# A redrawn order for a fused attention and channel-mix kernel: first v early, five idle matmul pairs, relu and square in one step

## The chip, the cores and the metric

The kernel runs on one core of a Trainium2 chip. The metric is the time of one execution on the device in microseconds. A profile of one execution shows what each engine did: PE is the tensor engine (PEld its weight loads), DVE the vector engine, ACT the scalar engine, POOL the GpSimd engine and SP the sync engine, which here only issues DMAs.

## What is computed

Chunked attention feeds a channel mix. For 8 batches, 8 heads, 576 positions and head width 64, attention runs inside chunks of 64 positions:

```python
scores = scale * q_c @ k_c^T;  scores -= max;  attn = exp(scores);  attn /= sum + 1e-9
x = (attn @ v_c), heads side by side          # (8, 576, 512)
```

The channel mix then works on x, with x_prev the position before (zero at the start of a batch):

```python
xk = mu_k * x + (1.0 - mu_k) * x_prev
xr = mu_r * x + (1.0 - mu_r) * x_prev
k = np.maximum(xk @ w_k, 0.0)                 # w_k is 512 x 1024
v = k * k @ w_v                               # w_v is 1024 x 512
r = 1.0 / (1.0 + np.exp(-(xr @ w_r)))         # w_r is 512 x 512
return (r * v).astype(np.float32)
```

The weights arrive as 64-bit floats and are turned into 32-bit ones on the chip.

## The kernel before

The 4608 positions (8 times 576) are 18 groups g of 256. For each group the kernel loads q, k and v, turns q and k so that the head width lies on the partitions, computes scores and softmax, transposes the probabilities, multiplies them with v (which gives x already turned), mixes neighbouring positions, and forms the products with w_r, w_k and w_v. Large products are computed in f32 accuracy from two parts: each operand is split into a rounded high part and a low rest (`rounded` tiles), and three products of the four are added up (PASSES). For groups 0 to 3 these are plain products; groups 4 to 17 go in pairs p = 2 to 8 whose product with w_k (task M, tiles m) and with w_v (task V, tiles o) each take seven block products instead of eight, with sums and differences on DVE around them.

Nothing schedules the program: every step has a name, and a string ORDER of some two thousand words gives the order in which all of them are issued, with the engine behind a colon where there is a choice (A for ACT, D for DVE, G for POOL's queue). A second table, PLACE, gives each tile its address. Every engine works through its own steps in that order and waits by semaphores for the others. The words that the text uses:

- nk and nq load k and q of the first groups (lines 469 and 486), bq and bk those of later ones (531), v the values (501), sw the weights (581).
- T turns q and k on PE (tiles trq and trk, lines 649 and 673); their copies from PSUM run on ACT (line 415) or DVE (417).
- S is scores and softmax of the first groups (PE 724; maximum 746, exponential on ACT 762), Z the softmax of later groups (788 to 813, the last step at 813).
- P transposes the probabilities (tiles pt, line 841), copies them and multiplies with v (xps, 854).
- cw are the four steps that convert a block of weights: two on ACT (lines 585 and 589), two on DVE (592 and 598). hw splits it.
- Mk and Mr mix in groups 0 to 3 (938), R is the product with w_r (pr, 1140), K that with w_k (pk, 1094), V that with w_v (pv, 1173, and o, 1498).
- E is relu and square of k (lines 1075 to 1083); in the pairs these are blocks c11, c21, c22 and c12. F splits the result (1452).
- W.0 and W.1 clear a tile and run three matmuls of 512 columns on it at the start; W.2 to W.9 are FILL = 8 further steps of two idle matmuls each (line 440). Their results are used by nothing.

Of the kernel before, what the change touches and what calls it, by code (L numbers as in the profile page):

```python
# [12 lines left out]
ALU = mybir.AluOpType  # L13
# [10 lines left out]
mu.0:A nk0.0 P0.3:D W.0:D W.1 nq0.0 nk0.1:A nq0.1 nk1.0:A mu.1 T0.6 nq1.0:A mu.2:A T0.0 T0.8:A  # L24
T0.7:D T0.9 T0.2:A T0.1:D T0.3 T0.11:D T0.10:A S0.0 S0.1:D T0.5:A T0.4:A S0.2:D S0.3:A S1.0 T1.3
T1.4:A T1.5:A S1.1:D S1.2:D S1.3:A S0.4:D S0.5:D W.2 W.4 W.3 T1.0 P0.0 W.5 swr0.0 S1.4:D S1.5:D v0.0
swr1.0 cwr0.1:A T1.2:A cwr0.0:A P0.1:A T1.1:A cwr0.2:D W.6 P1.0 P0.2 dg.3 dg.1 dg.0 dg.2 v1.0 nk2.0
nq2.0 v2.0 P1.1:A cwr0.3:D S2.0 S3.0 P0.4:A cwr1.0:A cwr1.1:A S2.1:D S2.2:D Mk0.0 T2.3 P1.2 Mr0.0
swk0.0 v3.0 S2.3:A hwr0.0:A S3.1:D cwr1.2:D P1.3:D S3.2:D Mk0.1:A P1.4:A S3.3:A S2.4:D S2.5:D
Mk0.2:D T2.5:A P2.0 T2.4:A P2.1:A Mr0.1:A cwr1.3:D S3.4:D Mr0.2:D S3.5:D P2.3:D hwr1.0:A T2.0 P2.2  # L30
Mk1.0 cwk0.1:A P2.4:A cwk0.0:A T2.2:A Mk1.1:A hwr1.1:D hwr0.1:D cwk0.2:D cwk0.3:D P3.0 Mr1.0 P3.1:A
T2.1:A Mr1.1:A Mr1.2:D P3.3:D Mk1.2:D Mk2.0 hwk0.0:A P3.2 S4.0 S5.0 swk2.0 P3.4:A cwk2.0:A cwk2.1:A
hwk0.1:D Mr2.0 W.7 R01.0 swk1.0 Mk3.0:D S5.1:D Mk3.1:D cwk2.2:D Mk2.1:A cwk1.0:A cwk1.1:A S5.2:D
Mr3.0:D cwk1.2:D cwk1.3:D hwk1.0:D hwk1.1:D Mk2.2:D R01.1:A R00.0 swk3.0 bq3.1 swv3.0 bk3.0 bq3.3
bk3.1 swv0.0 Mr3.1:A cwk3.1:A cwk3.0:A R00.1:A Mr2.1:A K00.0 cwv3.1:A K00.1:A bq3.2 bk3.3 cwk3.2:D
# [286 lines left out]

PLAIN, ROUNDED = 16384, 40064
FIRST = 2
FILL = 8


class Steps:
# [1301 lines left out]
```

## Time and profile before

| | us |
|---|---|
| runs | 588.2, 586.47, 587.41 (median 587.41) |
| profiled execution | 584.91, of which the span is 583.1 |
| PE busy | 562.2 (96%) |
| DVE busy | 523.0 (90%) |
| ACT busy | 410.9 (70%) |
| POOL busy | 227.8 (39%) |

The profiled execution is one more run; its span leaves 1.8 us around it. Busy time of an engine counts instructions, not the issue of DMAs. Matmuls overlap in the engine's pipeline, so a busy PE is not PE at its peak. A releaser behind an idle time is the event that came last before the engine went on.

### The profile page before, as it was taken

To read this page: it belongs to the slowest core of one execution; us is meant where nothing else is said; L and a number is where in the kernel's file an instruction comes from. 1 tells how busy PE (TensorE), PEld (TensorE's weight loads), DVE (VectorE), ACT (ScalarE), POOL (GpSimd) and SP (SyncE) were. 2 spreads that over 40 slices of the span, in tenths; PEclk is the share of its full clock that TensorE was granted. 3 is DMA by queue.
4 is the path that set the end of the run, shared out by engine and by line. 5 is a ranking of instruction groups with operands and counts; after the bars stand their busy time and mean duration, and the time that the engine had idled before them with its cause. 6 is when DMAs were issued, how large, how long until landed. Compare 5 with 4: busy or idle time off the path is not lost.

```text
span 583.1 us, 16267 instructions
## 1 busy us (share of the span) xinstructions
PE 562.2 (96%) x6215; PEld 522.6 (90%) x6215; DVE 523.0 (90%) x878; ACT 410.9 (70%) x813; POOL 227.8 (39%) x410
## 2 busy tenths in 40 slices
PE   6889999999999999998999999999999999999996
PEld 4788998898888999997999899999998999999996
DVE  1899999889989999969998999989989998988784
ACT  2899877585675897867866875877768866946451
POOL 2400042111000035586446744257476456474710
PEclk9999999999999999999999999999999999999999
DMA  9797643443265667999769966899698746374721
GB/s 214 203 295 204 183 87 64 86 105 80 47 166 140 195 145 179 245 237 194 147 143 214 250 129 158 160 176 231 140 268 177 163 114 160 93 178 98 187 80 73
DMA packets 211453, 93.38 MB, mean 160 GB/s; under 512 B 162024, under 2 KB 201968, under 8 KB 211376
## 3 DMA queue, kind: packets, MB, share of 16 engines
q0 software_dynamic: 45824, 49.05, 33.9%
q1 hardware_dynamic: 160544, 41.46, 33.3%
q10 hardware_dynamic: 5008, 1.84, 1.5%
q8 instruction: 49, 0.80, 0.6%
q14 instruction: 28, 0.23, 0.1%
HBM read 76.55 MB, written 15.73 MB: 158 GB/s over the span
## 4 chain that ended last, share of the span: by engine, by line
PE 63%; DVE 13%; SPq 10%; DMA 6%; issue 4%; ACT 2%; POOL 1%; ACTq 1%; DVEq 0%; POOLq 0%
PE o L1498 23%; PE m L1408 12%; PE pr L1140 11%; SPq L531 8%; PE pk L1094 5%; PE pv L1173 4%; PE s L724 2%; DMA plain<-in_k 2%; PE xps L854 2%; PE pt L841 2%; DVE rounded L1452 2%; DVE plain L1422 1%; DVE plain L699 1%; DVE plain L1460 1%; SPq L529 1%
## 5 line engine op out<-in xcount | busy, mean ns | idle before, releaser
L1315 POOL DMA_DIRECT2D rounded<-kept x288 | 156.2, 549 | 153.9 <-PE pr L1140 88.3
L1498 PE MATMUL o<-rounded 128*128 128x256 f32 x1176 | 150.0, 285 | 2.7 <-DVE rounded L1452 2.3
L1498 PEld LDWEIGHTS o<-rounded 128*128 128x128 f32 x1176 | 144.2, 191 | 5.1 <-DVE rounded L1452 2.9
L1408 PE MATMUL m<-rounded 128*128 128x256 f32 x1176 | 147.4, 284 | 0.2 <-DVE plain L1422 0.2
L1408 PEld LDWEIGHTS m<-rounded 128*128 128x128 f32 x1176 | 143.7, 192 | 1.8 <-DVE plain L1422 0.6
L415 ACT ACTIVATE rounded<-plain 128x512 fp32r<-128x512 f32 (+1 forms) x158 | 100.6, 663 | 28.1 <-DVE plain L1034 9.1
L1140 PE MATMUL pr<-rounded 128*128 128x512 f32 x432 | 103.5, 392 | 0.4 <-ACT plain L1077 0.3
L501 POOL DMA_DIRECT2D plain<-in_v x76 | 47.8, 631 | 134.0 <-DMA plain<-in_k 55.5
L1140 PEld LDWEIGHTS pr<-rounded 128*128 128x128 f32 x432 | 79.5, 188 | 17.0 <-DVE rounded L1055 0.5
L1017 ACT ACTIVATE plain<-xps,mu 128x256 f32<-128x256 f32 x128 | 54.6, 490 | 21.8 <-PE xps L854 16.8
L1452 DVE TENSOR_TENSOR rounded<-plain,rounded 128x512 fp32r<-128x512 f32 x98 | 65.1, 681 | 2.0 <-PE o L1498 1.2
L1023 ACT ACTIVATE plain<-xps,mu 128x255 f32<-128x255 f32 (+3 forms) x176 | 62.5, 451 | 5.2 <-DMA out<-plain 4.7
L1173 PE MATMUL pv<-rounded 128*128 128x512 f32 x192 | 48.4, 398 | 0.7 <-DVE rounded L1116 0.7
L1094 PEld LDWEIGHTS pk<-rounded 128*128 128x128 f32 x384 | 47.2, 192 | 0.7
L699 DVE STREAM_TRANSPOSE plain<-plain 128x512 f32<-128x512 f32 x60 | 41.4, 699 | 7.1 <-DMA plain<-in_q 6.9
L1094 PE MATMUL pk<-rounded 128*128 128x256 f32 x384 | 47.6, 283 | 0.0
L1083 ACT ACTIVATE plain<-plain 128x512 f32<-128x512 f32 x64 | 39.5, 631 | 8.4 <-DVE plain L1075 7.8
L1034 DVE TENSOR_TENSOR plain<-plain 128x512 f32<-128x512 f32 x64 | 42.8, 678 | 0.4 <-ACT plain L1023 0.2
L1173 PEld LDWEIGHTS pv<-rounded 128*128 128x128 f32 x192 | 34.8, 188 | 8.2 <-DVE rounded L1116 1.5
L1460 DVE TENSOR_TENSOR plain<-plain 128x512 f32<-128x512 f32 x56 | 38.2, 687 | 1.5 <-ACT plain L1083 0.7
L415 ACT ACTIVATE plain<-m 128x512 f32<-128x512 f32 x42 | 24.2, 604 | 16.7 <-PE m L1408 13.6
L1422 DVE TENSOR_TENSOR plain<-m,plain 128x512 f32<-128x512 f32 x42 | 28.4, 681 | 6.4 <-PE m L1408 6.2
(103 smaller groups left out, 735.7 us busy)
## 6 DMA issues: line engine op xcount, KB each, us to landing
rounded<-kept POOLq DMA_DIRECT2D x288, 128.0 KB, 3.3
kept<-rounded SPq DMA_DIRECT2D x12, 512.0 KB, 3.6
out<-plain POOLq DMA_DIRECT2D x24, 256.0 KB, 3.2
plain<-in_q SPq DMA_DIRECT2D x160, 32.0 KB, 2.9
plain<-in_k SPq DMA_DIRECT2D x160, 32.0 KB, 2.4
plain<-in_v POOLq DMA_DIRECT2D x76, 64.0 KB, 2.7
plain<-in_v SPq DMA_DIRECT2D x68, 64.0 KB, 3.7
plain<-in_moe_w_k SPq DMA_DIRECT2D x4, 1024.0 KB, 6.4
```

What stands on the lines that cost most here:

```text
L415: nc.scalar.activation(to, x, AF.Copy)
L501: queue(on).dma_start(out=vt[j * CH : (j + 1) * CH, :, e, :], in_=v[b, j * HP : (j + 1) * HP, c * CH : (c + 1) * CH, :].rearrange("h t d - ...
L699: nc.vector.transpose(out=x, in_=x)
L1017: nc.scalar.activation(now(nm, h)[:, c], xps()[:, cb], AF.Copy, scale=mu2[:, 0, i, cb : cb + 1])
L1023: nc.scalar.activation(before(nm)[:, cb, s : s + n], xps()[:, cb, s - 1 : s - 1 + n], AF.Copy, scale=mu2[:, 1, i, cb : cb + 1],)
L1094: nc.tensor.matmul(pk[:, e, :], wk_at(f // 4)[:, a, cb, f % 4 * P : (f % 4 + 1) * P], x[:, b, cb, :], start=(n == 0), stop=(n == 3 * NB - 1),)
L1140: nc.tensor.matmul(pr, xr_at(g, a, cb)[:, tl * TT : (tl + 1) * TT], wr_of(g, cb // 2)[:, b, cb % 2, :], start=(n == 0), stop=(n == 3 * NB ...
L1173: nc.tensor.matmul(pv, kk_at(g, a, f // 2)[:, f % 2, tl * TT : (tl + 1) * TT], wv_at(f // 4)[:, :, b, f % 4, :], start=(f == 0 and n == 0) ...
L1315: nc.gpsimd.dma_start(out=to[:, c : c + 256], in_=of[:, c : c + 256])
L1408: nc.tensor.matmul(ps[w][:, e, :], left(n, a, cb, 2 * u + e), right(g, n, b, cb), start=first and i == 0, stop=i == 11, skip_group_check=True,
L1452: engine[e].tensor_tensor(form(p, n, u, 1), r(i), f32(form(p, n, u, 0)), ALU.subtract)
L1498: nc.tensor.matmul(ps[w][:, tl, :], form(p, n, u, a)[:, e, tl * TT : (tl + 1) * TT], moving(n, b, 2 * u + e), start=first and i == 0, stop ...
```

## The change

ORDER and PLACE are drawn anew throughout; of ORDER's table the diff shows the first line of either kernel. FILL goes from 8 to 5, so the steps W.7 to W.9 are gone. Relu and square of c11, c21 and c22 become one step `relu2`: on DVE one instruction that takes the maximum with 0 and multiplies with the tile itself, on ACT two activations, one behind the other. The block c12 keeps relu (out of PSUM) and square as two steps. Of the 42 such steps 32 run on ACT and 10 on DVE; before, 29 of the relus ran on ACT and 13 on DVE, and 37 of the squares on ACT and 5 on DVE. In c12, relu goes from 11 on ACT and 3 on DVE to 12 and 2, and square from 13 and 1 to 10 and 4. Elsewhere, steps with a choice change engine in both directions. All in all DVE has 880 instructions for 878, and ACT 779 activations for 791. Lines of the body are 6 lower up to relu2, 1 higher from there and 4 higher behind the pairs' relu step.

```diff
-mu.0:A nk0.0 P0.3:D W.0:D W.1 nq0.0 nk0.1:A nq0.1 nk1.0:A mu.1 T0.6 nq1.0:A mu.2:A T0.0 T0.8:A
...
+W.0:D W.1 mu.0:A nk0.0 nq0.0:A nk0.1 nq0.1:A v0.0 T0.6 mu.1 nk1.0 T0.7:D T0.8:D T0.0 P0.3:D T0.2:D
...
-FILL = 8
+FILL = 5
...
+    def relu2(e, x):
+        if e == "D":
+            nc.vector.scalar_tensor_tensor(out=x, in0=x, scalar=0.0, in1=x, op0=ALU.max, op1=ALU.mult)
+        else:
+            relu(e, x, x)
+            square(e, x)
+
...
         for i in ("c11", "c21", "c22", "c12"):
 
             def f_relu(e, i=i):
-                relu(e, r(i), ps[0] if i == "c12" else r(i))
+                relu(e, r(i), ps[0])
 
             def f_sq(e, i=i):
                 square(e, r(i))
 
             do.task = f"E{i}_{p}{u}"
-            do(f_relu, "AD")
-            do(f_sq, "AD")
+            if i == "c12":
+                do(f_relu, "AD")
+                do(f_sq, "AD")
+            else:
+                do(lambda e, i=i: relu2(e, r(i)), "AD")
 
```

The first place is the opening. SP's queue issues the loads; its first ten rows before are (in_k, in_q, in_v, in_moe_w_r are the inputs):

```order
L486 DMA plain<-in_k 64x4x128 x2
L486 DMA plain<-in_q 64x4x128 x4
L581 DMA plain<-in_moe_w_r 128x2x1024
L501 DMA plain<-in_v 64x4x64 x4
L581 DMA plain<-in_moe_w_r 128x2x1024
L501 DMA plain<-in_v 64x4x64 x4
L486 DMA plain<-in_k 16x4x256 x2
L486 DMA plain<-in_k 48x4x256 x2
L486 DMA plain<-in_q 16x4x256 x2
L486 DMA plain<-in_q 48x4x256 x2
```

and now:

```order
L480 DMA plain<-in_k 64x4x128 x4
L495 DMA plain<-in_v 64x4x64 x4
L463 DMA plain<-in_k 128x8x64 x2
L575 DMA plain<-in_moe_w_r 128x2x1024
L480 DMA plain<-in_k 16x4x256 x2
L480 DMA plain<-in_k 48x4x256 x2
L575 DMA plain<-in_moe_w_r 128x2x1024
L495 DMA plain<-in_v 64x4x64 x4
L480 DMA plain<-in_q 16x4x256 x2
L480 DMA plain<-in_q 48x4x256 x2
```

The first loads of v (line 501, now 495) stand directly behind the first of k, ahead of the first piece of w_r (581, now 575); the first loads of q went to ACT's queue, and the two pieces of w_r lie further apart.

On ACT, the stretch from the first exponentials (line 762, now 756) to the copies of the probabilities of group 0 (pt_0) reads before (trk and trq are turned k and q, 585 and 589 the conversion of w_r, now 579 and 583; the last number in a name counts buffers):

```order
L762 ACTIVATE plain_70<-plain_70 128x512
L415 ACTIVATE plain_70<-trk0_1_223 128x4x128
L415 ACTIVATE plain_70<-trk1_1_228 128x4x128
L762 ACTIVATE plain_70<-plain_70 128x512
L589 ACTIVATE plain_70<-plain_70 128x1024
L415 ACTIVATE plain_70<-trq1_1_258 128x4x128
L585 ACTIVATE plain_70<-plain_70 128x1024
L415 ACTIVATE plain_70<-pt_0_263 128x512
L415 ACTIVATE plain_70<-trq0_1_253 128x4x128
L415 ACTIVATE plain_70<-pt_0_263 128x512
```

and now:

```order
L756 ACTIVATE plain_70<-plain_70 128x512 x2
L409 ACTIVATE plain_70<-trk0_1_231 128x4x128
L409 ACTIVATE plain_70<-trk1_1_236 128x4x128
L409 ACTIVATE plain_70<-trq1_1_264 128x4x128
L409 ACTIVATE plain_70<-pt_0_274 128x512
L583 ACTIVATE plain_70<-plain_70 128x1024
L579 ACTIVATE plain_70<-plain_70 128x1024
L409 ACTIVATE plain_70<-xps_0_291 128x4x128
```

The two conversions, which stood ahead of the copy of pt_0, stand behind it, and the copy of trq0_1 is no longer among ACT's rows here.

The second place is the transposes of group 4's probabilities (pt_4, rows of line 841, now 835) on PE. Before (pk and pv are products with w_k and w_v of the group named by the first number, warm6 is an idle pair):

```order
L1094 MATMUL pk_2_3_1709<-rounded_71 128x256 x24
L440 MATMUL warm6_1734<-plain_70 128x128 x2
L1173 MATMUL pv_2_0_1737<-rounded_71 128x512 x6
L1173 MATMUL pv_2_1_1744<-rounded_71 128x512 x9
L1094 MATMUL pk_3_1_1758<-rounded_71 128x256 x24
L1173 MATMUL pv_2_0_1737<-rounded_71 128x512 x3
L841 MATMUL pt_4_1803<-ident_72,plain_70 128x128 x4
L1173 MATMUL pv_2_1_1744<-rounded_71 128x512 x3
L841 MATMUL pt_4_1803<-ident_72,plain_70 128x128 x4
```

and now (pr is the product with w_r):

```order
L1141 MATMUL pr_2_0_1614<-rounded_71 128x512 x12
L1141 MATMUL pr_2_1_1673<-rounded_71 128x512 x12
L1095 MATMUL pk_2_3_1706<-rounded_71 128x256 x24
L1174 MATMUL pv_2_0_1741<-rounded_71 128x512 x3
L1174 MATMUL pv_2_1_1745<-rounded_71 128x512 x6
L1174 MATMUL pv_2_0_1741<-rounded_71 128x512 x3
L1095 MATMUL pk_3_0_1758<-rounded_71 128x256 x24
L835 MATMUL pt_4_1791<-ident_72,plain_70 128x128 x8
```

The idle pair is gone, the products with w_r of group 2 stand nearer to the transposes, and all eight transposes come together. Ahead of the first of them PE has 1018 matmuls, where it had 1028.

On DVE, the softmax that those transposes wait for ends with the row of line 813 (now 807; zg_4 holds group 4's sums and their reciprocals). Before:

```order
L1208 TENSOR_TENSOR plain_70<-rounded_71 128x512
L1214 TENSOR_TENSOR plain_70<-plain_70 128x512
L807 TENSOR_REDUCE zg_4_1784<-plain_70 128x16
L808 TENSOR_SCALAR zg_4_1784<-zg_4_1784 128x16
L809 RECIPROCAL zg_4_1784<-zg_4_1784 128x16
L1007 TENSOR_TENSOR plain_70<-last_2_1376,mu2_78 128x4
L813 TENSOR_TENSOR plain_70<-plain_70,zg_4_1784 128x1024
```

and now:

```order
L1237 TENSOR_TENSOR rounded_71<-plain_70,rounded_71 128x512
L693 STREAM_TRANSPOSE plain_70<-plain_70 128x4x128
L801 TENSOR_REDUCE zg_4_1737<-plain_70 128x16
L802 TENSOR_SCALAR zg_4_1737<-zg_4_1737 128x16
L803 RECIPROCAL zg_4_1737<-zg_4_1737 128x16
L1117 TENSOR_TENSOR rounded_71<-plain_70,rounded_71 128x512
L411 CAST rounded_71<-plain_70 128x512
L807 TENSOR_TENSOR plain_70<-plain_70,zg_4_1737 128x1024
```

Two steps of other groups stand between the reciprocal and the last step, where there was one. Up to and with that last step DVE has 179 instructions, where it had 172.

## Rows read from the trace of the kernel before

**Rows 1.** The page, part 1: busy time, share and instructions of an engine.
```profile
PE 562.2 (96%) x6215; PEld 522.6 (90%) x6215; DVE 523.0 (90%) x878; ACT 410.9 (70%) x813; POOL 227.8 (39%) x410
```

**Rows 2.** By stretch: length, busy time (instructions) of each engine, PEclk, DMA share, GB/s.
```profile
5.87:12.40 6.53, 2.81 (x128) 2.53 (x131) 1.28 (x3) 2.64 (x6) 1.96 (x4) 0.95 1.18 281
...
30.00:44.10 14.10, 12.70 (x267) 11.83 (x268) 12.87 (x20) 14.10 (x19) 0.00 (x0) 1.00 0.96 311
44.10:100.00 55.90, 55.90 (x464) 50.42 (x463) 54.14 (x81) 47.13 (x76) 10.10 (x16) 1.00 0.57 136
100.00:133.00 33.00, 33.00 (x329) 29.76 (x328) 28.59 (x47) 21.73 (x43) 4.96 (x8) 1.00 0.43 89
133.00:275.00 142.00, 136.57 (x1492) 124.78 (x1491) 132.54 (x228) 103.49 (x219) 43.55 (x77) 1.00 0.69 163
275.00:447.00 172.00, 169.50 (x1927) 160.69 (x1925) 163.09 (x280) 126.31 (x264) 94.94 (x173) 1.00 0.88 182
447.00:578.40 131.40, 131.34 (x1278) 126.62 (x1278) 115.28 (x197) 82.51 (x170) 63.73 (x116) 1.00 0.53 128
```

**Rows 3.** What PE waits for from 44 us on: total us, times, longest.
```profile
PE o L1498 <- DVE rounded L1452: 2.3, 3, 1.9
PE xps L854 <- DMA plain<-in_v: 1.1, 1, 1.1
```

**Rows 4.** Timeline of the opening: start, duration, engine, line, operation, tiles, [idle before].
```profile
8.73 1.28 ACT L550 ACT_TABLE_LOAD   x1 [8.73 <-DMA plain<-in_k]
...
10.32 0.63 PE L673 MATMUL trq<-ident,plain 64*64 64x64 f32 x27 [3.65 <-ACT mu L551]
...
12.47 2.20 PE L724 MATMUL s<-plain 64*64 64x64 f32 x63
...
17.12 1.13 ACT L589 ACTIVATE plain<-plain 128x1024 int32<-128x1024 uint32 x1
...
19.46 0.60 PE L841 MATMUL pt<-ident,plain 128*128 128x128 f32 x4
...
20.15 1.12 ACT L585 ACTIVATE plain<-plain 128x1024 f32<-128x1024 f32 x1
21.18 0.58 ACT L415 ACTIVATE plain<-pt 128x512 f32<-128x512 f32 x1
...
23.16 1.16 PE L724 MATMUL s<-plain 64*64 64x64 f32 x64
...
43.77 0.61 PE L440 MATMUL warm<-plain 128*128 128x128 f32 x4
...
44.14 2.09 PE L1140 MATMUL pr<-rounded 128*128 128x512 f32 x8
```

**Rows 5.** PE's clock by stretch of 1 us, columns as in rows 2.
```profile
12.00:13.00 1.00, 1.00 (x50) 1.00 (x46) 0.00 (x0) 0.19 (x1) 0.79 (x2) 0.50 1.09 313
...
14.00:15.00 1.00, 1.00 (x30) 0.88 (x23) 0.97 (x3) 0.00 (x0) 0.45 (x2) 0.50 1.35 218
```

**Rows 6.** PE's timeline around the idle matmuls of W.8 and the transposes of group 4.
```profile
123.40 0.61 PE L440 MATMUL warm<-plain 128*128 128x128 f32 x4
123.77 3.69 PE L1173 MATMUL pv<-rounded 128*128 128x512 f32 x15
...
130.87 0.60 PE L841 MATMUL pt<-ident,plain 128*128 128x128 f32 x4
```

**Rows 7.** DVE's timeline: the last step of group 4's softmax.
```profile
127.99 1.22 DVE L813 TENSOR_TENSOR plain<-plain,zg 128x1024 f32<-128x1024 f32 x1
```

**Rows 8.** Groups by line: instructions, busy time, mean ns of one.
```profile
L417 DVE CAST rounded<-plain 128x512 fp32r<-128x512 f32 (+1 forms) x69 | 29.8, 436 | 1.2 <-PE o L1498 0.7 <-ACT plain L1083 0.2
...
L592 DVE SCALAR_TENSOR_TENSOR plain<-plain 128x1024 int32<-128x1024 int32 x10 | 12.2, 1220 | 1.1 <-ACT plain L585 1.1
...
L1075 DVE TENSOR_SCALAR plain<-plain 128x512 f32<-128x512 f32 x13 | 5.6, 434 | 0.1
...
L1081 DVE TENSOR_TENSOR plain<-plain 128x512 f32<-128x512 f32 x8 | 5.5, 684 | 0.1
```

More of the change, by code (lines that the diff above doesn't have):

```diff
@@ L319 @@
-o22_8:14848 o12_8:0
+idle:0 warm:0 warm0:3 warm1:1 warm2:0 warm3:3 warm4:2 mu_t:1 diag_k0:5120 diag_k1:5632 diag_r0:6656
+diag_r1:6144 natk0:15360 natq0:14336 natk1:12800 natq1:11776 natk2:7168 natq2:10752 st_wr0:3072
+st_wr1:1024 st_wk0:11776 st_wk1:0 st_wk2:9728 st_wk3:2048 st_wv0:0 st_wv1:2048 st_wv2:8192
+st_wv3:4096 wr0:6144 wr1:4096 wk0:10240 wk1:14336 wv0:24576 wv1:19968 trq00_0:0 trq01_0:2 q0:9728
+trq10_0:2 trq11_0:0 trk00_0:2 trk01_0:3 k0:10752 trk10_0:1 trk11_0:3 v0:13824 v1:512 p0:14848
@@ new lines @@
+p1:14336 pT0:14848 pT1:14336 x0:15360 x1:8192 mxk_0:2 xk_0:0 mxr_0:3 xr_0:2048 mxk_1:1 mxr_1:3
+pk_0_0:0 r_0_0:14336 kk00_0:19456 kk10_0:28672 pk_0_1:3 r_0_1:12800 kk01_0:18432 kk11_0:18944
+pk_0_2:2 r_0_2:12800 kk02_0:29184 kk12_0:30720 pk_0_3:1 r_0_3:13312 kk03_0:19456 kk13_0:33792
+pr_0_0:3 sg_0:11776 pr_0_1:2 pv_0_0:1 pv_0_1:2 trq0_1:1 trq1_1:0 q1:11776 trk0_1:2 trk1_1:3 k1:12800
+v2:0 v3:9216 p2:13824 p3:14848 pT2:14336 pT3:14848 x2:15360 x3:14848 mxk_2:0 xk_1:8192 mxr_2:1
+xr_1:2048 d3:15872 mk3:13824 mr3:13312 pk_1_0:0 r_1_0:13312 kk00_1:24064 kk10_1:0 pk_1_1:0
@@ new lines @@
+c12_40:15360 f100_4:4096 f101_4:33792 f200_4:32256 f201_4:29184 f400_4:24064 f401_4:5120
+f500_4:37888 f501_4:4096 f700_4:38400 f701_4:38912 f600_4:4096 f601_4:38912 f300_4:29184
+f301_4:35840 m0_4_1:3 c11_41:6656 m1_4_1:2 m2_4_1:1 c22_41:0 c21_41:9216 c12_41:6144 f110_4:38912
+f111_4:33792 f210_4:28672 f211_4:39424 f410_4:5632 f411_4:37376 f510_4:4608 f511_4:18432
+f710_4:28672 f711_4:38400 f610_4:37888 f611_4:31744 f310_4:38912 f311_4:1024 o0_4:1 o11_4:8704
+o1_4:3 o2_4:2 o22_4:3072 o12_4:6656 k10:13824 q10:3584 v20:2560 v21:4608 p_10:14336 pT20:5632
@@ new lines @@
+pT21:15360 bk_10:14336 ak0_10:15872 ak1_10:14336 xk_10:0 br_10:3072 ar0_10:8192 ar1_10:14848
+xr00_10:37888 xr10_10:39424 xr01_10:38400 xr11_10:32256 k11:8192 q11:9728 v22:2048 v23:2560
+p_11:8192 pT22:5120 pT23:15360 bk_11:1536 ak0_11:15360 ak1_11:9216 br_11:13312 ar0_11:5120
+ar1_11:14848 xr00_11:18432 xr10_11:36864 xr01_11:1536 xr11_11:35840 raw3_5:6144 t30_5:1024
+t31_5:37376 t10_5:0 t11_5:35840 t20_5:24064 t21_5:36352 b220_5:36864 b221_5:0 t40_5:24064
+t41_5:37376 wr0_5:6144 wr1_5:33792 tv50_5:32768 tv51_5:27648 tv60_5:26624 tv61_5:31744 tv70_5:37888
@@ new lines @@
+c22_80:13824 c21_80:14336 c12_80:15872 f100_8:34304 f101_8:24064 f200_8:28672 f201_8:38912
+f400_8:35840 f401_8:36352 f500_8:25600 f501_8:37376 f700_8:36864 f701_8:32256 f600_8:38400
+f601_8:38912 f300_8:34816 f301_8:5632 m0_8_1:2 c11_81:8704 m1_8_1:1 m2_8_1:1 c22_81:15360
+c21_81:11264 c12_81:9216 f110_8:34816 f111_8:36864 f210_8:36864 f211_8:34816 f410_8:35328
+f411_8:37888 f510_8:39424 f511_8:32256 f710_8:38400 f711_8:32768 f610_8:37376 f611_8:34304
+f310_8:37376 f311_8:38912 o0_8:0 o11_8:9728 o1_8:3 o2_8:1 o22_8:14848 o12_8:15872
```

548 lines of the change are left out of this document (257 added, 291 removed).

## The prediction, made before the changed kernel was run

> **What bounds the kernel now.** I read the page's busy shares first, then busy time by stretch, then what the tensor engine waits for, and last the timeline of the opening, because the first three say that little else is left to win. The shares [rows 1] are to show that TensorE is the bound: 562.2 us of the 583.1 us span, with VectorE second at 523.0 and ScalarE far behind at 410.9. The stretches [rows 2] say where TensorE's missing 20.9 us lie. From 44.1 us on it is idle 5.43 us between 133 and 275, 2.50 us between 275 and 447 and 0.06 us from there to its last product at 578.4: 8.0 us in all. The 4.7 us after 578.4 hold no product. So some 8 us are lost before 44.1, and that is the stretch whose order the change redraws most. The waits after 44 us [rows 3] are small single events, the largest 2.3 us in three pieces on VectorE's split (line 1452) and 1.1 us on a load of v. Nothing there is a rhythm that a new order would remove everywhere.
>
> The opening's timeline [rows 4] is to be read as a chain. ScalarE waits for its first work until 8.73, loads a table for 1.28, and the first scores start at 12.47. The first transposes of the probabilities (pt, group 0) stand at 19.46, but ScalarE copies the first half of them only at 21.18, since two conversions of w_r (1.13 at line 589, 1.12 at line 585) are queued ahead. The next scores (23.16) stand behind that copy and the one of the second half. From 30 to 44.1 ScalarE is busy 14.10 of 14.10 us [rows 2]: there it sets the pace, until the first product with w_r at 44.14.
>
> **The opening, part by part.** The ACT rows of the order show that both conversions now stand behind the pt copy, and that one query copy (trq0_1) has gone to VectorE. The time that they took ahead of the copies, 1.13 + 1.12 = 2.25 us, leaves the chain. Ahead of that, three or four more turned tiles are copied by VectorE, which is busy only 1.28 of 6.53 us there [rows 2], and a first idle matmul pair no longer stands in front of the transposes. ScalarE's start after the table load stays, since the two query loads are still issued from it; I put the first scores at 11.5 instead of 12.47, 1.0 us. Sum 3.3 us. The ends are 0 (ScalarE has the same conversions to do somewhere before 44, and it is full from 30 on) and 5.0 (those two and three further instructions of 0.6 us that went to VectorE). I take 3.3, because what ScalarE loses ahead of the copies it must do only before the products that use it.
>
> The loads: v of group 0 stands ahead of w_r on SyncE's queue, and the second k block and the second weights piece come after it, so w_r lands later by four loads. Its conversion is wanted later too, which hides this. Over the whole run eight v loads go from SyncE to GpSimd's queue and seven come back. GpSimd is busy 227.8 of 583.1 us [rows 1], so I cost it at nothing; if a v load came late, the one wait of this kind in the trace is 1.1 us [rows 3], and that much can be lost or won.
>
> **Three idle pairs less.** The pair W.7 holds TensorE from 43.77 to 44.14, 0.37 us from start to start [rows 4]; W.8 from 123.40 to 123.77, 0.37 us too [rows 6]. W.7 lies in the opening, where TensorE isn't the bound, and counts nothing of its own. W.8 and W.9, the latter by estimate the same, stand between products: -0.7 us. Ends: 0, if TensorE waits there anyway, and -1.1, if all three count.
>
> **Relu and square.** On VectorE 13 relus in place of 434 ns and five squares of 684 ns [rows 8] become ten single instructions. No row shows this form at 128x512 in f32: half of the 1220 ns of the same operation on 1024 columns of integers is 610, the whole is 1220, and the square, which also reads two operands, is 684. I take 0.68 as the nearest. 13 x 0.434 + 5 x 0.684 = 9.06 against 10 x 0.68 = 6.8: -2.3 us. In the c12 blocks one relu goes to ScalarE and three squares come: about 1.4 us back, so -0.9. But the order has seven more casts on VectorE (7 x 0.436 = +3.05) and other moves that about cancel; VectorE's sum grows by some 2 us, from 878 instructions to 880. Its idle time, 60 us over the span, is what hides this; uncovered, it would cost those 2 us. Were the new instruction at 1220 ns, ten would add 5.4 us, and that too would go into the idle time unless it falls in a full stretch. ScalarE falls from 791 to 779 activations (table loads apart); from 44 us on it is free by more than 20% in every stretch but the first [rows 2], so this wins nothing. I cost the edit at 0, with ends -1 and +2.2.
>
> **The redrawn order after the opening.** The price here is VectorE's lead. The first transposes of group 4 (pt_4) start at 130.87 on TensorE [rows 6] and need VectorE's last softmax step, which ends at 127.99 + 1.22 = 129.21 [rows 7]: 1.66 us of room. Counted in the order up to that step, VectorE has 179 instructions where it had 172, and TensorE reaches pt_4 after 1018 matmuls instead of 1028. Seven at 0.68 [rows 8] are 4.8 us, and ten matmuls at 0.12 to 0.24 (15 in 3.53 us [rows 6]) some 1.8. VectorE must run 4.8 + 1.8 - 1.66 = 4.9 us further ahead. Four of the seven are copies in the opening, where it stands idle, worth some 2.2 us; the other 2.7 must come out of its idle time between 44.1 and 133, which is 1.76 + 4.41 = 6.2 us [rows 2]. Behind pt_4 TensorE has the products of group 2 with w_v queued, and they would wait with it. Ends: 0 and 4.9; I take 1.0, since most of the idle time can be used. The 8.0 us of waits after 44 I leave as they are: ends -8 and, were they to double, +8; a different order loses some and makes others.
>
> **The sum**, against the profiled execution (584.91 us, of which 583.1 are span): -3.3 - 0.7 + 0 + 1.0 = -3.0, so 581.9. The profiled run is 2.5 us below the median of the timed ones, 587.41; with the same 0.43% on top that is 584.4. What a measurement of this kernel can tell from no change is about 0.3%, here 1.76 us: 585.65 and 589.17 are the bounds.
>
> **The rivals.** (A) The new order also heals waits: of the 8.0 us half go. For it: they are single events, and one of VectorE's is a wait for a load of q that now stands earlier. Against it: a new order makes new ones. -7.0, so 580.4.
> (B) The opening's gain is given back: from 44.1 to 100 VectorE is busy 54.14 of 55.90 us [rows 2], with the weights' low parts to make just in time for the products that use them. If they come when they came before, TensorE waits 3.3 us for them. -0.7 + 1.0 is nothing, about 587.7. Against it: VectorE too starts that stretch earlier.
> (C) Slower: VectorE is the bound from the opening to group 4. It arrives at the softmax step of pt_4 at before's time plus the seven instructions, 129.21 + 4.8 = 134.0; TensorE, which had 130.87 there and has 1.8 us less to do ahead, loses 134.0 - 130.87 + 1.8 = 4.9 us, the opening's lead is swallowed, and W.9 alone is won (0.4): +4.5, so 591.9. It decides where VectorE arrives less than 2.7 us earlier than so. For it: the 97% of that stretch. Against it: the 6.2 us of idle time and the copies that lie in the opening.
> (D) The clock. Between 12 and 15 us the granted clock is 0.50 [rows 5], that is 1.2 GHz, behind 3.65 us in which TensorE waited, until 10.32, for ScalarE's first work [rows 4]; from 44.1 on it is 1.00 in every stretch [rows 2]. A pair that is left out can lengthen such idle time, and one more dip of those 3 us at half clock would cost 1.5 us where TensorE is the bound: 585.9. Against it: the dip falls where ScalarE sets the pace. The Trainium skill, page "TensorE: Matmul & The Clock Gate", section "Part 1: The HAM clock gate", says that the throttled state is the default and that activity releases it, so that fewer idle matmuls speak against this change; by that rule the time would be 585.9, by the row with its one dip 584.4. That a dip follows idle time is what the trace shows; that leaving out a pair brings one, no row of it shows.
>
> **How the numbers follow.** The forecast as summed 0.40, with a range of its own from 582.5 to 586; A 0.15; B 0.21; C 0.19; D 0.05. Faster: 0.40 and 0.15, less 0.02 for the forecast's upper edge, 0.53. Same: B, D and that edge, 0.28. Slower: 0.19. The range that should hold 8 in 10 goes from 579.5, just under A, to 590, which takes in B whole and the weaker part of C.
>
> **What would show it.** In the profile after, the second scores should start near 20 (23.16 now), and the products with w_r and w_k some 3 us earlier; no conversion of w_r should stand between pt and its copy. TensorE's idle time from the first product on should be 8 to 9 us. If C holds, the waits name VectorE's softmax step ahead of pt near 128 us; if B, the low parts of the weights ahead of pk between 44 and 70; if D, PEclk falls under 0.9 in a second slice. The fused step should show 0.68 us; near 1.2 would refute its price. The prediction is wrong at its root if the span shortens by more than 8 us or VectorE's waits on TensorE's path grow by more than 5.

## The result, and the profile after

The changed kernel is slower: 590.39 us in the median of 20 runs (586.34 to 596.12) against 586.37 of 20 runs of the kernel before, a ratio of 1.0067 with a 95% interval of 1.0044 to 1.0091. Medians here are of all runs, while ratios leave out the few runs that lie well above the fastest of their kernel (two of these 20; in e5 one of seven, at 1094 us). Its profiled execution took 589.38 us, of which 587.5 are span, 4.47 more than the 584.91 of before.

The page's busy shares of the changed kernel answer to [rows 1]. They hardly differ: the same work is done, and TensorE's idle time is what grew.

```profile
PE 563.0 (96%) x6203; PEld 524.5 (89%) x6203; DVE 521.8 (89%) x880; ACT 406.1 (69%) x801; POOL 230.0 (39%) x414
```

By stretch of the changed kernel (columns as in [rows 2]):

```profile
44.10:100.00 55.90, 54.64 (x461) 49.47 (x460) 54.10 (x83) 49.32 (x82) 14.39 (x23) 1.00 0.61 159
100.00:133.00 33.00, 32.84 (x327) 29.61 (x326) 32.28 (x54) 24.47 (x48) 3.09 (x5) 1.00 0.44 93
133.00:275.00 142.00, 137.83 (x1511) 127.39 (x1510) 131.26 (x227) 102.84 (x216) 42.26 (x75) 1.00 0.65 151
275.00:447.00 172.00, 165.83 (x1890) 158.34 (x1889) 157.38 (x268) 118.72 (x254) 98.72 (x177) 0.98 0.86 179
447.00:578.40 131.40, 130.75 (x1266) 125.56 (x1266) 113.32 (x197) 83.75 (x168) 60.77 (x112) 1.00 0.56 133
```

TensorE's idle time in these five is 1.26, 0.16, 4.17, 6.17 and 0.65 us, together 12.4 where it was 8.0 [rows 2], and in the fourth the granted clock is no longer 1.00. The page's line of clocks over 40 equal slices shows where: the 28th slice, 396 to 411 us, is the only one past 30 us that falls.

```profile
PEclk9899999999999999999999999997999999999999
```

What TensorE waits for in the changed kernel, total, times and longest in us, answers to [rows 3]. These rows are of the whole run. The wait for ScalarE's copy of the transposed probabilities leads; past 44 us it is 4.6 us, where it was 0.6:

```profile
PE pt L835 <- ACT plain L409: 5.3, 3, 3.3
PE trk L643 <- DMA plain<-in_k: 2.2, 2, 1.5
PE m L1409 <- DVE plain L1423: 1.6, 1, 1.6
```

The longest, 3.3 us, is the one in that slice. The timeline of the changed kernel there (start, duration, engine, line, tiles, idle before), for TensorE and ScalarE:

```profile
395.48 0.60 PE L835 MATMUL pt<-ident,plain 128*128 128x128 f32 x4
...
396.23 0.67 ACT L409 ACTIVATE plain<-o 128x512 f32<-128x512 f32 x1
...
396.71 0.92 ACT L1011 ACTIVATE plain<-xps,mu 128x256 f32<-128x256 f32 x2
...
397.42 0.94 ACT L1017 ACTIVATE plain<-xps,mu 128x255 f32<-128x255 f32 x2
...
398.13 0.74 ACT L409 ACTIVATE rounded<-plain 128x512 fp32r<-128x512 f32 x1
...
398.65 0.71 ACT L409 ACTIVATE plain<-pt 128x512 f32<-128x512 f32 x1
...
399.42 1.11 PE L835 MATMUL pt<-ident,plain 128*128 128x128 f32 x4 [3.34 <-ACT plain L409]
...
400.19 5.39 PE L1502 MATMUL o<-rounded 128*128 128x256 f32 x24
```

TensorE transposes the first half of group 13's probabilities at 395.48 and then stands until 399.42 for the second half. What releases it is ScalarE's copy of the *first* half, 398.65, and ScalarE had a copy of a result, four steps of the mix and a split to do ahead of that. Both halves are one tile of PSUM, and a step that writes the tile is made to wait for a copy of it that stands earlier in the program, though the halves don't overlap (e1 and e2 move the step and the wait goes and comes). The order decides: now it reads "P26.0 Hr112.0:D O5.2:A Ak12.2:A Hr012.0:A P26.1:A ... P27.0". The kernel before has "P26.0 P27.0 ... P26.1:A", and its timeline shows the eight transposes in one go:

```profile
397.00 1.04 PE L841 MATMUL pt<-ident,plain 128*128 128x128 f32 x8
```

TensorE's granted clock in the same place, by stretches of 2 us (columns as in [rows 2], PEclk third from the end):

```profile
397.00:399.00 2.00, 0.00 (x0) 0.00 (x0) 2.00 (x4) 2.00 (x6) 2.00 (x4) 0.88 1.17 214
399.00:401.00 2.00, 1.58 (x8) 1.58 (x9) 0.09 (x1) 0.80 (x2) 1.83 (x5) 0.50 1.32 265
...
403.00:405.00 2.00, 2.00 (x11) 2.00 (x11) 1.62 (x3) 0.63 (x1) 0.55 (x2) 0.50 1.37 279
```

So the wait is paid for a second time. The four transposes took 1.11 us where the first four took 0.60, and the next 24 products 5.39 us, where the same 24 take 3.11 us at full clock in e1 below: 0.51 + 2.28 = 2.8 us. With the wait that is 6.1 us at one place, more than the whole loss of 4.47. Apart from it, the profiled execution would be 1.7 us ahead of before.

The opening of the changed kernel, to be read beside [rows 4]:

```profile
7.27 1.28 ACT L544 ACT_TABLE_LOAD   x1 [7.27 <-DMA plain<-in_q]
...
9.91 0.68 PE L718 MATMUL s<-plain 64*64 64x64 f32 x31
...
13.95 0.63 PE L643 MATMUL trk<-ident,plain 128*128 128x128 f32 x4 [1.46 <-DMA plain<-in_k]
...
18.78 1.03 PE L835 MATMUL pt<-ident,plain 128*128 128x128 f32 x4
...
22.05 0.65 PE L718 MATMUL s<-plain 64*64 64x64 f32 x32
23.51 0.70 PE L718 MATMUL s<-plain 64*64 64x64 f32 x32 [0.81 <-DVE m L740]
...
41.23 3.03 PE L1141 MATMUL pr<-rounded 128*128 128x512 f32 x12
...
48.62 1.59 PE L1095 MATMUL pk<-rounded 128*128 128x256 f32 x12
```

The first scores come at 9.91 for 12.47, 2.6 us sooner, of which the table load, done 1.46 us sooner, has a part. Then 1.46 us (and 0.74 again at 15.3) go to a wait for k of group 1, which now is loaded behind the first v. The transposes of group 0 come at 18.78 for 19.46, at a slow clock (granted 0.59 from 18 to 20 us; 1.03 us for four), and the next scores, which started at 23.16 in one piece, come in two, at 22.05 and 23.51. The first product with w_r comes 2.9 us sooner (41.23 for 44.14), but a step of the mix that stood ahead of it now stands behind it. The first product with w_k starts at 48.62, where the kernel before has:

```profile
49.69 1.48 PE L1094 MATMUL pk<-rounded 128*128 128x256 f32 x11
```

A lead of 2.6 us at the first scores is 1.1 us there.

The fused step of the changed kernel, by line (instructions, busy us, mean ns):

```profile
L1081 DVE SCALAR_TENSOR_TENSOR plain<-plain 128x512 f32<-128x512 f32 x10 | 6.7, 682 | 0.1
```

### The profile page after: what moved, and what is told of

Its sections match the earlier page's. It is cut to its first block, busy times and chain, and to the rows that moved or that the text cites. A ratio compares the mean times of both kernels' runs of the same rounds, so it can differ in the third digit from the quotient of the medians.

```text
span 587.5 us, 16232 instructions
## 1 busy us (share of the span) xinstructions
PE 563.0 (96%) x6203; PEld 524.5 (89%) x6203; DVE 521.8 (89%) x880; ACT 406.1 (69%) x801; POOL 230.0 (39%) x414
## 4 chain that ended last, share of the span: by engine, by line
PE 57%; DVE 13%; DMA 10%; ACT 8%; SPq 7%; issue 4%; POOL 1%; DVEq 0%; ACTq 0%; POOLq 0%
PE o L1502 18%; PE m L1409 17%; PE pr L1141 10%; PE pv L1174 6%; SPq L525 5%; DMA plain<-in_q 4%; DMA plain<-in_k 2%; PE pt L835 2%; PE xps L848 2%; ACT plain L409 2%; DMA plain<-in_moe_w_r 2%; PE s L718 2%; PE pk L1095 1%; ACT rounded L409 1%; DVE plain L693 1%
## 5 line engine op out<-in xcount | busy, mean ns | idle before, releaser
L1502 PEld LDWEIGHTS o<-rounded 128*128 128x128 f32 x1176 | 146.0, 195 | 3.3 <-DVE rounded L1049 1.5
L409 ACT ACTIVATE rounded<-plain 128x512 fp32r<-128x512 f32 (+1 forms) x151 | 96.6, 663 | 45.5 <-DVE plain L1368 18.0
L495 POOL DMA_DIRECT2D plain<-in_v x80 | 50.1, 629 | 192.2 <-DMA plain<-in_k 55.7
L1456 DVE TENSOR_TENSOR rounded<-plain,rounded 128x512 fp32r<-128x512 f32 x98 | 65.2, 680 | 10.6 <-PE o L1502 5.8
L1174 PE MATMUL pv<-rounded 128*128 128x512 f32 x192 | 46.4, 394 | 0.0
L1077 ACT ACTIVATE plain<-plain 128x512 f32<-128x512 f32 x57 | 35.6, 632 | 1.4 <-DVE plain L1069 0.2
L1049 DVE TENSOR_TENSOR rounded<-plain,rounded 128x512 fp32r<-128x512 f32 x50 | 33.9, 681 | 2.6 <-PE m L1409 1.3
```

What stands on the lines that cost most here:

```text
L409: nc.scalar.activation(to, x, AF.Copy)
L495: queue(on).dma_start(out=vt[j * CH : (j + 1) * CH, :, e, :], in_=v[b, j * HP : (j + 1) * HP, c * CH : (c + 1) * CH, :].rearrange("h t d - ...
L1174: nc.tensor.matmul(pv, kk_at(g, a, f // 2)[:, f % 2, tl * TT : (tl + 1) * TT], wv_at(f // 4)[:, :, b, f % 4, :], start=(f == 0 and n == 0) ...
L1456: engine[e].tensor_tensor(form(p, n, u, 1), r(i), f32(form(p, n, u, 0)), ALU.subtract)
L1502: nc.tensor.matmul(ps[w][:, tl, :], form(p, n, u, a)[:, e, tl * TT : (tl + 1) * TT], moving(n, b, 2 * u + e), start=first and i == 0, stop ...
```

## The experiments

Ratios are to the kernel before, run on the same chip in the same job, with 95% intervals. All edits are words of ORDER unless another line is shown.

**e1: the second half ahead of the copy of the first.** The changed kernel with

```diff
-P26.0 Hr112.0:D O5.2:A Ak12.2:A Hr012.0:A P26.1:A F_51.3:D Hr112.1:D D28.1:D P27.0 V2_5.1
+P26.0 P27.0 Hr112.0:D O5.2:A Ak12.2:A Hr012.0:A P26.1:A F_51.3:D Hr112.1:D D28.1:D V2_5.1
```

> The changed kernel with one word moved: the second half of group 13's transposes (P27.0) directly behind the first half (P26.0), ahead of the copy of the first half (P26.1) instead of behind it. Theory 1 (one tile, two halves): in the changed kernel TensorE stands 3.34 us at 396 because the second half writes a tile whose first half ScalarE has yet to copy, and runs at half clock until 405 behind it, together 6.2 us. Then the wait at 396 is under 0.5 us, the granted clock stays 1.00 from 395 to 411, and the ratio to the kernel before falls from 1.0067 to 0.996 (0.994 to 0.998), some 584 us. Theory 2 (ScalarE is overfull there: busy 13.28 of 13.40 us from 386 to 399.4): the products with v need the same copy, the wait moves there, and the ratio stays above 1.004.

Measured: 586.47 us, ratio 0.9998 (0.9971 to 1.0026). That interval lies wholly below the changed kernel's (1.0044 to 1.0091): one word carries the loss. The timeline of TensorE in e1 shows the place without a wait and at full clock, eight transposes and the 24 products:

```profile
398.55 1.04 PE L835 MATMUL pt<-ident,plain 128*128 128x128 f32 x8
399.34 3.11 PE L1502 MATMUL o<-rounded 128*128 128x256 f32 x24
```

From the first transpose to the next product with v (405.51 in the changed kernel, 402.38 in e1) it is 10.0 us in the changed kernel and 3.8 in e1, 6.2 us less; in e7 to e12, which have this move too, it is 3.8 or 3.9 each time. ScalarE is as full there as before the edit (busy 13.34 of 13.40 us from 386 to 399.4, and 13.28 before), and TensorE waits for nothing else there; theory 2 falls.

But the ratio is 0.9998 and not the 0.996 expected: what should have been left of the forecast gain isn't there in the median. In the profiled execution one can see where it went: e1's TensorE reaches the place 3.1 us later than the changed kernel's (398.55 against 395.48). Of these, 1.8 us are lost near 250, where TensorE waits for VectorE in both kernels, but in e1 with a slow clock behind the wait (granted 0.61 and 0.54 in the stretches from 252 and 254; 1.00 in the changed kernel). The same 48 products in the changed kernel and in e1:

```profile
249.56 6.02 PE L1409 MATMUL m<-rounded 128*128 128x256 f32 x48 [1.64 <-DVE plain L1423]
```

```profile
251.23 7.49 PE L1409 MATMUL m<-rounded 128*128 128x256 f32 x48 [2.00 <-DVE plain L1423]
```

**e2: the same word moved the other way in the kernel before.**

```diff
-P26.0 P27.0 F7_51.0:A F7_50.0:A F2_51.0:A P26.1:A O5.2:A
+P26.0 F7_51.0:A F7_50.0:A F2_51.0:A P26.1:A P27.0 O5.2:A
```

> The kernel before with the same word moved the other way: P27.0 behind the copy P26.1, as in the changed kernel. Theory 1: a new wait of TensorE for ScalarE's copy of pt appears near 391, as long as ScalarE's queue ahead of the copy (three splits of 0.6 us and the copy, 1 to 3 us); the ratio to before is 1.002 to 1.005, and above that if the clock falls. Theory 2 (the place of the word does nothing, ScalarE's load does): no new wait, ratio 1.000.

Measured: 585.81 us, ratio 0.9996 (0.9978 to 1.0015). The wait appears as theory 1 has it, but it is short, since ScalarE gets to its three splits early there:

```profile
398.19 0.66 PE L841 MATMUL pt<-ident,plain 128*128 128x128 f32 x4 [0.69 <-ACT plain L415]
```

The ratio that theory 1 gave with it, 1.002 to 1.005, is missed, and by the time alone theory 2's 1.000 would do as well; it is the new wait that decides. So the place of the word makes a wait, and what stands ahead of the copy on ScalarE makes its size: 0.69 us here, and no clock falls; 3.34 us in the changed kernel.

**e5: k of group 1 ahead of v.** The changed kernel with

```diff
-mu.0:A nk0.0 nq0.0:A nk0.1 nq0.1:A v0.0 T0.6 mu.1 nk1.0
+mu.0:A nk0.0 nq0.0:A nk0.1 nq0.1:A nk1.0 v0.0 T0.6 mu.1
```

> The changed kernel with the two natural loads of k of group 1 (nk1.0) ahead of the first four loads of v on SyncE's queue instead of behind them. Theory a (the opening's gain was lost to late k): TensorE's two waits for in_k at 13.95 and 15.32 (2.2 us) go, the dip of the clock from 16 to 20 shrinks, and the first product with w_k comes 1 to 2 us sooner than 48.6; ratio to the kernel before 1.0067 less 0.002 to 0.003. Theory b (from 26 on ScalarE and VectorE set the pace): the waits go, but the first product with w_k moves by less than 0.5 us and the time by less than 0.1%.

Measured: 591.35 us, ratio 1.0095 (1.0058 to 1.0132). The waits for k of group 1 go, and the first product with w_k starts 0.9 us sooner than in the changed kernel, a little under theory a's 1 to 2 us. Its ratio is missed: the time is no better than the changed kernel's.

```profile
47.74 2.44 PE L1095 MATMUL pk<-rounded 128*128 128x256 f32 x19
```

The 0.9 us are gone by 80 us. Group 2 has the same coupling as group 13, since P5.0 stands behind P4.1, and TensorE waits there for ScalarE's copy: 1.26 us in the changed kernel, 2.27 in e5. There TensorE comes 0.3 us sooner, and the copy comes 0.7 us later (79.07 against 78.34), because ScalarE has stood 0.68 us for a load of w_v. Behind the wait the granted clock is 0.56, and at 100 us e5 is 2.3 us behind the changed kernel. In e5, ScalarE's wait for the load, its copy, and then TensorE's second half:

```profile
74.95 2.24 ACT L579 ACTIVATE plain<-plain 128x1024 f32<-128x1024 f32 x2 [0.68 <-DMA plain<-in_moe_w_v]
...
79.07 0.60 ACT L409 ACTIVATE plain<-pt 128x512 f32<-128x512 f32 x1
...
79.73 0.66 PE L835 MATMUL pt<-ident,plain 128*128 128x128 f32 x4 [2.27 <-ACT plain L409]
```

**e6: idle pairs in the wait.** Nine idle pairs (FILL = 14, all nine in PSUM bank 3) between P26.0 and P27.0 of the changed kernel.

> The changed kernel with nine idle matmul pairs between P26.0 and P27.0, where TensorE stood 3.34 us; the wait itself is left as it is. If the slow clock behind the wait costs 2.7 of the 6.2 us there, as I read it, then the clock stays at 1.00 from 397 to 407, P27.0 starts where it did or up to 0.5 us later (nine pairs at 0.37 are 3.3 us), and the ratio falls from 1.0067 to 1.002 (1.001 to 1.004). If the slow clock only coincides and costs nothing that is not waited for anyway, the ratio stays at 1.006 to 1.007.

Measured: 593.22 us, ratio 1.0132 (1.0105 to 1.0159). It does not answer its question. The pairs took 6.77 us, 0.75 each and not the 0.37 that I had read from W.8: all nine write one bank, and eight times a pair waited for the one before it, 2.0 us in sum. A step of ScalarE's mix that needed nothing of theirs waited for them, so that the copy and the second half came later still, behind 2.66 us of real idle time, and the clock fell anyway (0.50 from 407 to 409; the 24 products took 4.08 us):

```profile
396.86 6.77 PE L435 MATMUL warm<-plain 128*128 128x128 f32 x36
...
403.66 0.84 ACT L1012 ACTIVATE plain<-xps,mu 128x256 f32<-128x256 f32 x2 [5.92 <-PE warm L435]
...
406.29 1.11 PE L836 MATMUL pt<-ident,plain 128*128 128x128 f32 x4 [2.66 <-ACT plain L410]
```

What the slow clock costs therefore rests on the same 24 products at either clock, above. The Trainium skill, page "TensorE: Matmul & The Clock Gate", section "HAM oscillation — how this bites in real kernels", tells of waits for DMAs that bring the throttled clock back, so that the work behind each wait starts slow. The trace agrees, with waits for another engine as well: behind 3.34 us of waiting for ScalarE the 24 products took 5.39 us instead of 3.11.

**e7: group 2 as well.** The kernel of e1 with P5.0 directly behind P4.0. It then also stands ahead of S5.5, so the second half of group 2 is transposed before its softmax is normalised.

```diff
-P4.0 hwv3.1:D ... S5.5:D K00.3:A ... P4.1:A K13.1:A K11.0 P5.0
+P4.0 P5.0 hwv3.1:D ... S5.5:D K00.3:A ... P4.1:A K13.1:A K11.0
```

> The kernel of e1 with the same move for group 2 as well: P5.0 directly behind P4.0, where the changed kernel has it behind the copy P4.1 and TensorE waits 1.42 us at 77.4 (3.4 us in e5). Theory: the wait at 77 goes, the place from which the opening's lead of 1.1 us is lost, and the ratio to the kernel before falls below e1's 0.9998 by 0.002: 0.9975 (0.995 to 1.000). Rival: VectorE and ScalarE are full from 44 to 100 anyway, so the products with w_v behind it wait instead and the ratio stays within 0.001 of e1's.

Measured: 587.81 us, ratio 1.0018 (0.9989 to 1.0047): no gain can be seen over e1, and the theory's 0.9975 lies outside the interval; whether it is within 0.001 of e1's, as the rival had it, the noise hides. In this profile TensorE is 0.6 us ahead of the changed kernel's at 200 us, by the starts of the same products in both traces, and then VectorE waits 5.32 us for a load and TensorE 5.00 us for VectorE; 27 products that would take some 3.5 us (24 took 3.11 in e1) take 5.95 behind it, at a granted clock of 0.50. First VectorE and TensorE of e7, then its clock in one of the stretches of 2 us:

```profile
249.78 0.71 DVE L693 STREAM_TRANSPOSE plain<-plain 128x512 f32<-128x512 f32 x1 [5.32 <-DMA plain<-in_v]
...
252.32 5.95 PE L1409 MATMUL m<-rounded 128*128 128x256 f32 x27 [5.00 <-DVE plain L1423]
```

```profile
252.00:254.00 2.00, 1.68 (x8) 1.68 (x9) 1.97 (x3) 0.00 (x0) 1.09 (x2) 0.50 1.45 283
```

It is the place near 250 again: the 48 products took 8.46 us here, 7.49 in e1 and 6.02 in the changed kernel, behind waits of 5.00, 2.00 and 1.64 us. The order and the loads around it are alike in the three. In e7 SyncE issued its loads of k there 1.1 us sooner than in e1 (241.67 for 242.78), and VectorE's turn started 1.1 us later (249.78 for 248.69): what varies is when the load lands. I read it as the load of bk9.1, issued only just in time; which load it was isn't shown.

**e8: all halves together, and k of group 1 early.** The kernel of e7 with P1.0 (and S1.5, which it needs) behind P0.0, P33.0 behind P32.0, and nk1.0 as in e5; group 2 as in e7.

> The kernel of e7 with P1.0 behind P0.0 and P33.0 behind P32.0, so that no late group has a copy between the two halves, and with the k loads of group 1 ahead of v (as in e5). Theory: the opening's lead grows to 2 us as in e5 and now is kept past 80 us: ratio 0.994 (0.991 to 0.998), some 583 us. Rival: the lead is given back between 44 and 130 us, to ScalarE and VectorE, and the ratio is e7's.

Measured: 586.42 us, ratio 1.0009 (0.9975 to 1.0043). The theory's 0.994 falls. In this profile the lead never grew: the first product with w_k starts at 48.68, as in the changed kernel, and not at e5's 47.74. And 5.7 us are lost against the changed kernel at the place that the prediction had named, where the transposes of group 4 wait 3.09 us for VectorE's last softmax step (0.16 in the changed kernel), with a clock of 0.50 behind the wait. But it isn't VectorE's own work that makes it late, and TensorE comes only 0.3 us sooner than in the changed kernel (129.66 against 129.96): ahead of the softmax's last steps VectorE has stood 2.99 us for a load of q, which SyncE issued some 2.5 us later than in the changed kernel. VectorE's turn of q there in the changed kernel, then the same turn and TensorE's pt_4 in e8:

```profile
124.47 0.71 DVE L693 STREAM_TRANSPOSE plain<-plain 128x512 f32<-128x512 f32 x1 [0.27 <-DMA plain<-in_q]
```

```profile
127.09 0.71 DVE L693 STREAM_TRANSPOSE plain<-plain 128x512 f32<-128x512 f32 x1 [2.99 <-DMA plain<-in_q]
...
132.75 1.94 PE L835 MATMUL pt<-ident,plain 128*128 128x128 f32 x8 [3.09 <-DVE plain L807]
```

**e3: the fused step alone.** The kernel before with `relu2` as in the changed one, on VectorE where a relu or its square was there (17 of 42), else on ScalarE.

```diff
-            do(f_relu, "AD")
-            do(f_sq, "AD")
+            if i == "c12":
+                do(f_relu, "AD")
+                do(f_sq, "AD")
+            else:
+                do(lambda e, i=i: relu2(e, r(i)), "AD")
```

> The kernel before with relu and square of c11, c21 and c22 fused as in the changed kernel (17 instructions on VectorE, 25 pairs of activations on ScalarE), its order else unchanged. As predicted, the edit by itself is worth nothing: 0.682 us an instruction on VectorE, 13 relus at 434 ns and five squares at 684 ns less, +2.5 us on VectorE, hidden by 60 us of idle time; ratio 1.000 (0.998 to 1.002). Rival: the relus lay on the path to the products with w_v, and two steps in one shorten it: 0.997 or less.

Measured: 588.16 us, ratio 1.0035 (1.0001 to 1.0069). There is no gain. The median lies above the range that was forecast, and the interval lies just above 1: a small cost is likelier than none, and hardly told from none.

**e4: five idle pairs alone.** The kernel before without W.7, W.8 and W.9.

```diff
-FILL = 8
+FILL = 5
```

> The kernel before with five idle matmul pairs, W.7 to W.9 left out. As predicted, 0.37 us each for W.8 and W.9: ratio 0.9988 (0.997 to 1.000). Rival D: a dip of the clock more, of 1.5 us: 1.0014 or more, with a slice of the granted clock under 0.9 past 44 us.

Measured: 588.06 us, ratio 1.0005 (0.9969 to 1.0040). The -0.7 us is too small to be seen, rival D's +1.5 us is not excluded by the time, but in the profiled execution the slices of the clock past 44 us are all 0.9 or more.

**e9: a late load sooner.** The kernel of e1 with bk9.1 and bk10.3 exchanged. The block of k then goes over v of group 7 before its last use, so a part of the output is another.

> The kernel of e1 with two loads of SyncE's queue exchanged: the last block of k of group 9 (bk9.1), issued at 242.8 there and waited for by VectorE's turn until 248.7, against a block of group 10 (bk10.3) issued some 18 us sooner. Theory (late loads behind a queue that waits for a buffer of v until 219): VectorE's wait of 2.7 us at 248.7 and TensorE's of 2.0 us at 251 go, with no dip of the clock near 252 in any run; ratio to the kernel before 0.996 (0.993 to 0.999), as e1 gave 0.9998. Rival: another block is then late by as much, or VectorE has no slack there either way: ratio 0.999 to 1.001.

Measured: 593.75 us, ratio 1.0085 (1.0043 to 1.0127). The load can't go sooner in this drawing of PLACE: its block shares addresses with that v, whose product TensorE has yet to do. Put ahead of it, the load waits on SyncE's queue until its other buffers are free (eight loads in 9.34 us, 4.87 in e1), and TensorE's product with v now waits 4.81 us for the load, with a slow clock behind it. SyncE and then TensorE of e9:

```profile
224.34 9.34 SPq L525 DMA_DIRECT2D plain<-in_k  x8
```

```profile
231.06 1.99 PE L848 MATMUL xps<-plain 64*64 64x64 f32 x64 [4.81 <-DMA plain<-in_k]
```

So the theory was not tested, and neither it nor the rival foresaw this time; what the run does show is that the late load had no slack to be moved into, and what 4.81 us of waiting do to the time.

**e10: e9 with P5.0 behind S5.5.**

> The kernel of e9 with P5.0 directly behind the last softmax step of its half (S5.5), ahead of the copy P4.1. If the wait at 77 us (1.4 us) lies on the path to the end, TensorE keeps the opening's lead to 130 us and the ratio falls by another 0.002 below e9's; if VectorE's softmax of group 4 sets the pace there, as e8 had it (3.1 us of wait at 129 for its last step), the wait only moves to pt_4 and the ratio is e9's within 0.001, or above it by 0.003 where the clock falls behind the longer wait.

Measured: 591.67 us, ratio 1.0075 (1.0044 to 1.0107), e9's within the noise. It has e9's wait too (5.1 us), and tells of P5.0 nothing that e11 doesn't.

**e11: both couplings undone.** The kernel of e1 with P5.0 directly behind S5.5 and ahead of P4.1.

> The kernel of e1 with P5.0 directly behind the last softmax step of its own half (S5.5), ahead of the copy P4.1, so that both waits of TensorE for a copy of the other half are gone (1.4 us at 77, 3.3 us at 396). Theory: TensorE keeps the opening's lead of about 1 us past 83 us; ratio to the kernel before 0.998 (0.995 to 1.000). Rival: the lead is only a wait for VectorE's softmax of group 4 later, ratio 1.000 (0.998 to 1.003) as e1.

Measured: 586.07 us, ratio 0.9976 (0.9940 to 1.0012), the lowest ratio of these kernels, and not clearly below the one before: it is the theory's 0.998, and the interval holds the rival's 1.000 as well. Group 2's transposes now go in one piece (first row). Then pt_4 waits again for VectorE's softmax (last row), the rival's place, but not for a TensorE that has come early: it comes at 130.10, 0.1 us later than in the changed kernel. VectorE has stood 2.27 us for the load of q (second row), and with the slow clock behind pt_4's wait (granted 0.56 from 132 to 134) 3.6 us are lost here against the changed kernel:

```profile
75.05 1.40 PE L835 MATMUL pt<-ident,plain 128*128 128x128 f32 x8
```

```profile
126.61 0.71 DVE L693 STREAM_TRANSPOSE plain<-plain 128x512 f32<-128x512 f32 x1 [2.27 <-DMA plain<-in_q]
...
132.27 1.94 PE L835 MATMUL pt<-ident,plain 128*128 128x128 f32 x8 [2.17 <-DVE plain L807]
```

**e12: e11 with v15 later.**

```diff
-v15.0 bq9.1 Y41.2 bk10.3
+bq9.1 Y41.2 bk10.3 v15.0
```

> The kernel of e11 with four loads of v (v15) three steps later in SyncE's queue, behind blocks of q and k (bq9.1, bk10.3), since the queue stands 12 us there until the buffer of v15 is free (217.8 in the changed kernel). Theory: those blocks go out before 218, the queue is some 3 to 5 us ahead at 242, VectorE's turn near 249 and TensorE's product near 251 (2.0 us in e1, 5.0 in e7) no longer wait; ratio to the kernel before 0.996 (0.992 to 0.999). Rival: the blocks' own buffers come free no sooner, so that the queue gains nothing and v15, 4 us later, holds TensorE at the product with v near 222: ratio 1.000 or more.

Measured: 591.99 us, ratio 1.0077 (1.0041 to 1.0114). One of the blocks goes out early, but then a store to `kept` (Y41.2) holds SyncE's queue until 223.54, v15 follows only at 226.6, and TensorE waits 4.25 us for it. SyncE and TensorE of e12:

```profile
210.41 1.81 SPq L525 DMA_DIRECT2D plain<-in_q  x4
223.54 0.34 SPq L1293 DMA_DIRECT2D kept<-rounded  x1
```

```profile
231.27 1.42 PE L848 MATMUL xps<-plain 64*64 64x64 f32 x29 [4.25 <-DMA plain<-in_v]
```

## Why the prediction was wrong, step by step

**The step that failed** is the redrawn order after the opening. I had its price between 0 and 4.9 us, took 1.0, and looked for it in VectorE's lead; the waits after 44 us I left at 8.0, and they came to 12.4. The price came from another pair of engines: TensorE for ScalarE, at 396 us, 6.1 us with its slow clock, and e1 shows that it is the place of one word. The order that I compared did show it (P27.0 behind P26.1), but I had asked of each product only what VectorE must have done by then, and not which copies had moved between two writes to one tile. The same wait is in the kernel before, in the opening of [rows 4]: pt at 19.46, its copy at 21.18, and behind it the second half, a row that I hadn't shown:

```profile
21.81 0.66 PE L841 MATMUL pt<-ident,plain 128*128 128x128 f32 x4 [0.79 <-ACT plain L415]
```

**A wait has two prices.** In rival D I had the clock fall for lack of idle pairs; it fell for waits. D's sign, a second slice under 0.9, came, and e4, with the pairs left out alone, doesn't have it past 44 us. The prediction priced a wait by its length alone, and each of the long ones here (3.34, 5.00, 4.81, 4.25 us) was followed by a stretch at 0.50.

**The opening** was to give 3.3 us, 1.0 of them up to the first scores. It gave 2.6 there, ScalarE's table load having moved by 1.46 us where I had it stay, and 1.1 at the first product with w_k. The size was off: k of group 1 comes late by 2.2 us behind v (I had named its block among those behind v and asked only what w_r loses), of which e5 brings back 0.9 at the product with w_k; and from 26 us to 44.1 ScalarE is busy 17.93 and VectorE 17.42 of 18.10 us in the changed kernel.

**VectorE's lead at pt_4**, rival C's mechanism, cost 0.16 us in the changed kernel, where I took 1.0 and C 4.9. The 2.2 us in e11 and 3.1 in e8 come from a load of q that VectorE waited for, not from its instructions. So C had the right sign, with another place and mechanism than what made the kernel slower, and that its 591.9 us lie close to the measured 590.39 is luck. Rival B's outcome, the gain given back, is what e1, e8 and e11 measure: with the one bad wait gone the kernel is where it was. B's mechanism isn't seen: no wait of pk for the weights' low parts stands in the changed kernel's list of waits. In the profiles it is loads that land late (of w_v near 75 us in e5, of q near 125 in e8 and e11, near 250 in e1 and e7).

**The fused step** costs 0.682 us, as taken (0.68), and wins nothing, as forecast; e3 leaves open whether it costs up to 0.7%. VectorE's busy time, which I had growing by some 2 us, fell by 1.2. **The idle pairs** were to win 0.7 us; e4 can't tell that from nothing.

**What stays open** is why e1 isn't 1.7 us ahead in the median, as its place would let one expect from the profiled execution of the changed kernel. The profiles show single executions, and in e1's the 3.1 us lost ahead of the place account for most of it; how often the other runs meet late loads isn't known, nor whether the new order's loads are later than the old one's: e9 and e12, which moved two of them, only made it worse. A rival that wasn't tested in the changed kernel is the fused step: e3's 0.35%, if real, is 2 us.

## What to carry to other kernels

When an order is redrawn, look at each tile that is written in pieces, and whether a read of one piece now stands between two writes: the wait is as long as the reader's queue at that point, and the engine that writes stands with all that is behind it. Count a wait of TensorE as long as those here twice: the four of 3.3 to 5.0 us each had a stretch at half clock behind it, which cost 2.8 us behind 3.34 and 2.4 behind 5.00, and in e1 it still cost 1.5 us behind 2.00. Where an engine waits for another, look at what the other has waited for: pt_4 in e8 and e11 names VectorE's softmax, and the cause is a load ahead of it. And before a transfer is moved ahead in a full queue, find out when its buffer comes free: in e9 and e12 two loads moved by a few places made TensorE wait more than 4 us.

## What the hardware showed that was not expected

Idle matmuls aren't a fixed price: a pair took 0.37 us from start to start at W.8 [rows 6] and 0.75 us in e6, where nine in a row write one bank and wait for each other. Kernels that are alike around a word differ in the wait there: TensorE waited 1.6, 2.0 and 5.0 us near 250 in the changed kernel, e1 and e7, and the load behind it landed sooner or later by as much as 2.8 us (VectorE's turn at 247.01, 248.69 and 249.78).
